# Decode attention on one core: one matmul for the score mask, one for a head's q block, and the q block written by VectorE

## The chip, the core and the metric

The kernel runs on one core of a Trainium2 chip. Its time is the device time of one execution in microseconds (us): the median of several runs. The matrix engine is TensorE (PE in the profile, its weight loads PEld), VectorE is DVE, ScalarE is ACT, GpSimd is POOL, and SyncE (SP) issues nearly all transfers.

## What is computed

Four sequences (B = 4), one new token each, go through attention over a cached window, a gated feed-forward layer, the same attention again, and the feed-forward layer again, all with the same weights. Cut to what matters:

```python
# D = 512, 32 query heads on 8 KV heads (rep = 4), head size 128, window W = 2048 of 8192, F = 1792
x = x + A(layernorm(x))
x = x + B(layernorm(x))
x = x + A(layernorm(x))
x = x + B(layernorm(x))

def A(x):
    q = (x @ wq).reshape(B, 1, 32, 128)
    k, v = the last 2048 rows of k_cache, v_cache, each KV head for 4 query heads
    p = softmax(q @ k^T * 128 ** -0.5)
    return (p @ v) @ wo

def B(x):
    return (sigmoid(x @ w_gate) * (x @ w_up)) @ w_down
```

The caches and weights are bfloat16. The two attention layers share K, V and the weights, so K (16 MB) is read once and stays on the chip until the second layer has used it; V, wq, wo and the feed-forward weights are read for each layer, apart from a few tiles that are kept.

## The kernel before

**Storage and transfers.** `arena` holds 50 slots of 512 KB, `side` one more. K takes 32 of them. Every load names a slot; a slot that is given back by its last reader is handed to the next load in a fixed list, and SyncE issues the loads in that order (`dma`, L401), each behind a semaphore wait for that reader. So a late matmul can hold up a load, and all loads behind it on SyncE's queue.

**Order of work.** Each step is recorded by `P.op` with an engine, a name, a planned duration and what it reads and writes. `_schedule` then orders the steps of each engine by a simulated time made from the planned durations (`c_dve(n)` is 130 + 1.04 n ns for VectorE, `c_act(n)` 180 + 0.833 n ns for ScalarE), so a change of a step's engine or duration may reorder others. From the second attention on (`P.chain`), TensorE keeps the order of the program; VectorE, ScalarE and GpSimd are still ordered by the planner. Steps that touch one PSUM bank from different engines wait for each other (`banks`).

**A head's scores.** `q_unit` makes the q block of a KV head: `qh` holds a head's q for 4 sequences and 4 query heads in 32 rows, and the block `qbd` needs it spread so that the group of 32 partitions `a` holds only its own columns, with zeros elsewhere. Before, four matmuls (L875), each against a window of `eyew` (an identity of 32 columns inside zeros), write four interleaved column sets of one PSUM bank (`CB`), and ScalarE copies the 256 columns to `qbd` as bfloat16 (L880). `softmax_unit` then writes the mask (L905): four matmuls of 32 output partitions each put -1e30 into the columns that do not belong to a row; sixteen score matmuls (L916) add onto it. VectorE takes the row maximum (`mx`, L929), swaps halves (L933), combines (L937, L941), and ScalarE does the exponential (L944). `turn_p` permutes the probabilities with a matmul (L957), copies them (ScalarE, L959) and transposes them (VectorE, L964).

**First attention** (`attn_first`): VectorE turns K in place first, four transposes of about 1.2 us for each head (`k_transpose`, L887); scores run two heads ahead of the product with V (`pv_unit`, L1006).

**Second attention** (`attn_second`): K is already turned. `qx(u)` calls `q_unit` for the u-th head, `score(u, between)` emits mask, `between` and scores, and gives the head's K slots back to the pool. The loop over u runs, for each head: product with V (`pv_wide`, L1088), permutation of the next head (L957), `back(u-1)` (L1123), mask and scores of head u+3, the row maximum of head u+2, `sum_up(u+1)` (L1064, L1066), `qx(u+4)` and the output projection (`wo_wide`, L1142). On VectorE each product with V is followed by `tv` (L1097), `rd` (L1102) and `sh` (L1104). GpSimd then makes `av` (L1106, L1109).

**The last feed-forward layer** (`glu`): 16 matmuls each for w_gate and w_up (L1379), the transposes (L1388), `gh` (L1406) and, against `hT`, the w_down matmuls (L1420) on three loads that are the last in the list; then a copy (L1431) and the store.

Of the kernel before, what the change touches and what calls it, by code (L numbers as in the profile page):

```python
# [278 lines left out]
def build(nc, A_x, A_k, A_v, A_wq, A_wo, B_wg, B_wu, B_wd, out, cfg=None):  # L279
# [23 lines left out]
    NR = 4 * REP  # L303
# [21 lines left out]
    with es:  # L325
        def sb(name, shape, dt):
            return es.enter_context(nc.sbuf_tensor(name, shape, dt))
# [7 lines left out]
        one, inv_d, sres, psm, nmax = (small[:, a:b] for a, b in ((0, 1), (1, 2), (2, 4), (4, 6), (6, 12)))  # L335
        s3, msk_m = small[:, 12:15].bitcast(BF16), small[:, 15:16].bitcast(BF16)
        maskp, lnr, lnd, lnv, msks = (small[:, a:b] for a, b in ((16, 20), (20, 28), (28, 32), (32, 36), (36, 58)))
        eyew = sb("eyew", [128, 224], BF16)
        perm = sb("perm", [128, 128], BF16)
        sel_b = sb("sel_b", [128, NR], BF16)  # L340
        sel_r = sb("sel_r", [128, 2 * REP], F32)
        maskr = sb("maskr", [128, 32], F32)
        msk_s = sb("msk_s", [128, 32], BF16)
        rinv = sb("rinv", [128, 2 * NR], F32)
        onb = sb("onb", [128, 2 * NR], BF16)
        onp = sb("onp", [128, 2 * REP * NR], BF16)
# [45 lines left out]
        def c_dve(n, rate=None):  # L392
            return tm["dve_fix"] + n * (tm["dve_f32"] if rate is None else rate)

        def c_act(n):
            return tm["act_fix"] + n * tm["act_el"]
# [247 lines left out]
                                       base=0, channel_multiplier=-1),  # L644
             r=[("ones_f",)], w=[("e", 0)])
        P.op("gpsimd", "inv_d", 100.0, lambda g: g.memset(inv_d[:], 1.0 / D), w=[("inv_d",)])
        P.op("gpsimd", "eyew0", 200.0, lambda g: g.memset(eyew[:], 0.0), w=[("eyew0",)])
        P.op("vector", "zero_o", 1100.0, lambda v: v.memset(ps[:, OBS[0]:WB + 1, :], 0.0), w=[("o0",)], banks=OBS + (WB,))
        P.op("vector", "zero_perm", 100.0, lambda v: v.memset(perm[:], 0.0), w=[("perm",)])
        P.op("gpsimd", "qbd0", 1800.0, lambda g: g.memset(qbd[:], 0.0), w=[("q", k2) for k2 in range(2)])  # L650
# [1 line left out]
        for jh in range(2):  # L652
            for bp in range(2):
                for i in range(2):
# [7 lines left out]
                         r=[("ones_f",), ("e", 0), ("perm",)], w=[("perm", jh, bp, i)])  # L662
        perms = [("perm", jh, bp, i) for jh in range(2) for bp in range(2) for i in range(2)]
        P.op("gpsimd", "msk_s", 200.0,
             lambda g: g.affine_select(msk_s[:, :].rearrange("p (i y) -> p i y", i=2),
                                       ones_f[:, :].rearrange("p (i y) -> p i y", i=2),
                                       [[1, 2], [0, NR]], ALU.is_equal, 0.0, base=-1, channel_multiplier=1),
             r=[("ones_f",), ("e", 0)], w=[("msk_s",)])
        P.op("vector", "msk_s2", 100.0, lambda v: v.tensor_scalar(msk_s[:, :], msk_s[:, :], -1.0e30, None, ALU.mult),
             r=[("msk_s",)], w=[("msk_s",)])  # L670
# [9 lines left out]
             lambda v: v.tensor_reduce(sel_r[:, :], sel_f[:, :].rearrange("p (g y) -> p y g", g=2), AXX, ALU.add),  # L680
             r=[("sel_f",), ("e", 0)], w=[("sel_r",)])
        P.op("vector", "eyew", 200.0,
             lambda v: v.tensor_reduce(eyew[:, 96:128], ident.rearrange("p (a j) -> p j a", a=4), AXX, ALU.max),
             r=[("e", 0), ("eyew0",)], w=[("eyew",)])
        P.op("vector", "maskp", 200.0,
             lambda v: v.tensor_reduce(maskp[:, :], ident.rearrange("p (a j) -> p a j", a=4), AXX, ALU.max),
             r=[("e", 0)], w=[("maskp",)])
        P.op("vector", "maskb", 100.0,
             lambda v: v.tensor_reduce(maskb[:, :], maskp[:, :].rearrange("p (j b) -> p b j", j=2), AXX, ALU.max),
             r=[("maskp",)], w=[("maskb",)])  # L690
        ey = eyew[:, 96:128]
        P.op("vector", "maske", 100.0,
             lambda v: v.tensor_reduce(maske[:, :], ey.rearrange("p (e m) -> p e m", m=REP), AXX, ALU.max),
             r=[("eyew",)], w=[("maske",)])
# [5 lines left out]
                                       mod4[:, :].unsqueeze(2).broadcast_to([128, REP, 2]),  # L700
                                       maskp[:, 0:2].unsqueeze(1).broadcast_to([128, REP, 2]), ALU.mult),
             r=[("mod4",), ("maskp",)], w=[("selm",)])
        P.op("vector", "selw", 100.0, lambda v: v.tensor_copy(selw[:, :], eyew[:, 96:96 + NB]), r=[("eyew",)], w=[("selw",)])
        P.op("vector", "permo", 500.0,
             lambda v: v.tensor_copy(permo[:, :].rearrange("p (m r v) -> p m r v", m=REP, r=REP),
                                     ident.rearrange("p (v m) -> p m v", m=REP).unsqueeze(2).broadcast_to([128, REP, REP, 32])),
# [159 lines left out]

        def q_unit(tag, h, k2):
            hh = h % 4
            src = qh[32 * hh:32 * hh + 32, h // 4 * 64:h // 4 * 64 + 64].rearrange("p (x r) -> p x r", r=REP)
            dst = ps[:, CB, 0:256].rearrange("p (x y) -> p x y", y=NR)  # L870

            def e_qx(pe):
                last = None
                for a in range(4):
                    last = pe.matmul(dst[:, :, a * REP:(a + 1) * REP], eyew[32 * hh:32 * hh + 32, 96 - 32 * a:224 - 32 * a],  # L875
                                     src, start=True, stop=True)
                return last
            P.op("tensor", "qx" + tag, 250.0, e_qx, r=[("qh", h // 4), ("eyew",)], w=[("cb",)], banks=(CB,))
            P.op("scalar", "qe" + tag, c_act(256),
                 lambda a: a.copy(qbd[:, k2 * 256:(k2 + 1) * 256], ps[:, CB, 0:256]),  # L880
                 r=[("cb",)], w=[("q", k2)], banks=(CB,))

        def k_transpose(h):
            need(("K", h))
# [9 lines left out]
        def softmax_unit(tag, hk, wait=False, q=True, between=None):  # L894
            u = ucount[0]
            ucount[0] += 1
            k2 = u % 2
            bank, pt = {HKV: (OBS[0], 2), HKV + 1: (WB, 3)}.get(u, (SB[k2], k2))
            if q:
                q_unit(tag, hk, k2)  # L900

            def e_m(pe):
                last = None
                for gi in range(4):
                    last = pe.matmul(ps[32 * gi:32 * gi + 32, bank, :], msk_s[:, :],  # L905
                                     msk_m[:, :].unsqueeze(1).broadcast_to([128, 256, 2]), start=True, stop=False)
                return last

            def e_s(pe):
                last = None if wait else e_m(pe)  # L910
                for cp in range(4):
                    for gi in range(4):
                        jh, bp = gi // 2, gi % 2
                        kt = kpair(hk, bp).rearrange("p (j c k t) -> p c t j k", c=2, k=32, t=2)
                        q0 = ((k2 * 4 + cp) * 2 + bp) * 32
                        last = pe.matmul(ps[32 * gi:32 * gi + 32, bank, :], qbd[:, q0:q0 + 32],  # L916
                                         kt[:, cp // 2, cp % 2, jh * NJ:(jh + 1) * NJ, :], start=False, stop=(cp == 3))
                return last
            if wait:
                P.op("tensor", "M" + tag, 4 * tm["pe_row"], e_m, r=[("msk_s",), ("msk_m",)], w=[("pss", pt)], banks=(bank,))  # L920
                if between is not None:
                    between()
            P.op("tensor", "S" + tag, (16 if wait else 20) * tm["pe_row"], e_s,
                 r=[("msk_s",), ("msk_m",)] + [("slot", 4 * hk + t) for t in range(4)] + [("q", k2)],
                 w=[("pss", pt)], banks=(bank,))
            def soft():
                mk = mxt[:, k2 * 32:(k2 + 1) * 32]
                P.op("vector", "mx" + tag, c_dve(512),
                     lambda v: v.tensor_reduce(nmax[:, k2:k2 + 1], ps[:, bank, :], AXX, ALU.max),  # L929
                     r=[("pss", pt)], w=[("mx", k2)], banks=(bank,))  # L930
# [305 lines left out]
        def attn_second():  # L1236
# [8 lines left out]
            def qx(u):  # L1245
                if u < HKV:
                    q_unit(tag(u), hs[u], u % 2)

            def score(u, between=None):
                if u >= HKV:  # L1250
                    return
                softmax_unit(tag(u), hs[u], True, False, between)
                if u == 0:
                    soft(0)
                for bp in range(2):
                    pool.release(4 * hs[u] + 2 * bp)
                fill()
# [5 lines left out]
            def sum_up(u):  # L1263
                if u < NW:
                    sums(tag(u), u % 2)
                elif u < HKV:
                    sums_old(tag(u), u % 2)

            qx(0)
            score(0, lambda: q_mms(1, 0, OBS[1], (1,)))  # L1270
            qx(1)
            score(1)
            turn(0)
            qx(2)
# [299 lines left out]
```

## Time and profile before

| what | value |
|---|---|
| runs of the kernel before | 177.63, 177.19, 177.51 us; median 177.51 |
| the profiled execution | 177.0 us, of which the profile's span is 175.3 |
| busy share of the span | PE 60%, DVE 60%, ACT 19%, POOL 13% |
| loads | 70.00 MB, mean 399 GB/s |
| instructions on PE | 1661 matmuls and 1661 weight loads |

The span runs from the first instruction to the last of one execution; 1.7 us of that execution's own time lie around it. The profiled execution is 0.5 us shorter than the median of the runs. A busy share is a mean over stages with different limits; a row such as "L905 PE MATMUL" belongs to line 905 of the kernel before.

### The profile page before, as it was taken

The numbers are of one execution on the slowest core, as the hardware profiler recorded it, in microseconds if no ns is written. First come the engines' busy times: TensorE is split into PE (matmuls) and PEld (weight loads), VectorE is DVE, ScalarE is ACT, GpSimd is POOL, SyncE is SP. The second block draws the span as 40 slices with busy tenths as digits, with TensorE's granted clock in tenths as the row PEclk, the third lists the DMA queues.
The fourth block names the chain that finished last, engine by engine and source line by source line (L and its number), as shares of the span: only waits on it lengthen the run. The fifth ranks groups of instructions, "written<-read, shape, count | busy, mean of one in ns | idle before, by whom it ended". The sixth has DMA issues, their size and how long they took to land.

```text
span 175.3 us, 3927 instructions
## 1 busy us (share of the span) xinstructions
PE 105.7 (60%) x1661; PEld 54.7 (31%) x1661; DVE 104.4 (60%) x257; ACT 32.7 (19%) x87; POOL 22.2 (13%) x90
## 2 busy tenths in 40 slices
PE   0536246259566273661765456547977999776673
PEld 0203112014334041340445452142322444445321
DVE  6307997994957738378322381316299999751351
ACT  2002031322303003021030000100143455430011
POOL 6100010101101001010010000000011453442000
PEclk9999999999999999999999999999999999995555
DMA  5999999999999999999999999999999999999980
GB/s 188 426 426 426 426 419 424 408 421 423 419 419 412 420 424 426 421 405 427 419 419 415 415 400 407 402 410 403 394 413 404 423 419 424 421 416 423 419 344 25
DMA packets 12226, 70.00 MB, mean 399 GB/s; under 512 B 1320, under 2 KB 1328, under 8 KB 6064
## 3 DMA queue, kind: packets, MB, share of 16 engines
q1 hardware_dynamic: 12200, 69.74, 97.1%
q8 instruction: 13, 0.21, 0.5%
q14 instruction: 5, 0.04, 0.1%
q10 hardware_dynamic: 8, 0.00, 0.0%
HBM read 69.73 MB, written 0.00 MB: 398 GB/s over the span
## 4 chain that ended last, share of the span: by engine, by line
DMA 52%; DVE 24%; PE 19%; issue 2%; SPq 1%; ACT 0%; DVEq 0%
DMA arena<-in_A_v_cache_dram 20%; DMA arena<-in_B_w_down_dram 18%; DVE arena L887 12%; DMA arena<-in_A_wq_dram 10%; PE ps L916 8%; DMA arena<-in_B_w_gate_dram 5%; DVE small L929 3%; PE ps L905 3%; PE ps L1088 2%; DVE small L933 1%; DVE arena L593 1%; PE ps L1006 1%; DVE side L937 1%; PE ps L828 1%; DVE small L941 1%
## 5 line engine op out<-in xcount | busy, mean ns | idle before, releaser
L887 DVE STREAM_TRANSPOSE arena<-arena 128x1024 f32<-128x1024 f32 x32 | 37.0, 1205 | 0.1
L1006 PE MATMUL ps<-side,arena 128*128 128x8 bf16 x576 | 18.2, 168 | 14.1 <-DMA arena<-in_A_v_cache_dram 14.0
L916 PE MATMUL ps<-arena,side 128*32 128x512 bf16 x256 | 25.0, 524 | 0.1
L1006 PEld LDWEIGHTS ps<-side,arena 128*128 128x128 bf16 x576 | 16.7, 104 | 20.5 <-DMA arena<-in_A_v_cache_dram 18.8
L929 DVE TENSOR_REDUCE small<-ps 128x1 f32<-128x512 f32 x16 | 10.8, 676 | 17.6 <-PE ps L916 17.5
L944 ACT ACTIVATE side<-ps,small 128x512 bf16<-128x512 f32 x16 | 11.0, 687 | 36.8 <-PE ps L1024 18.3
L905 PE MATMUL ps<-small,msk_s 128*32 128x512 bf16 x64 | 8.4, 512 | 13.9 <-DVE arena L887 13.1
L880 ACT CAST side<-ps 128x256 bf16<-128x256 f32 x16 | 5.9, 370 | 34.4 <-PE ps L916 25.4
L959 ACT CAST side<-ps 128x512 bf16<-128x512 f32 x16 | 9.4, 586 | 10.8 <-PE ps L957 10.8
L916 PEld LDWEIGHTS ps<-arena,side 128*32 128x32 bf16 x256 | 8.2, 119 | 10.0 <-issue 7.2
L973 POOL CAST small<-small 128x1 bf16<-128x1 f32 x9 | 1.7, 188 | 76.1 <-ACT side L944 76.1
L957 PE MATMUL ps<-side,perm 128*128 128x512 bf16 x16 | 7.9, 494 | 5.2 <-ACT side L944 5.2
L828 PE MATMUL ps<-arena,xn 128*4 128x512 bf16 x60 | 7.5, 572 | 3.9 <-DMA arena<-in_A_wq_dram 3.6
L784 ACT ACTIVATE small<-ps 128x4 f32<-128x4 f32 x4 | 0.7, 174 | 48.1 <-PE ps L780 48.1
L1379 PE MATMUL ps<-arena,xn 128*4 128x448 bf16 x60 | 7.2, 549 | 3.3 <-DMA arena<-in_B_w_up_dram 1.5
L964 DVE STREAM_TRANSPOSE side<-side 128x256 f32<-128x256 f32 x16 | 6.9, 433 | 2.0 <-ACT side L959 1.8
L875 PE MATMUL ps<-side,eyew 32*128 32x64 bf16 x64 | 5.6, 217 | 3.4 <-ACT side L880 2.4
L1088 PE MATMUL ps<-arena,side 128*32 128x512 bf16 x112 | 7.3, 381 | 0.2 <-DVE small L941 0.2
L1014 DVE TENSOR_TENSOR onb<-ps,rinv 128x16 bf16<-128x16 f32 x9 | 1.7, 185 | 9.0 <-PE ps L1006 8.8
L905 PEld LDWEIGHTS ps<-small,msk_s 128*32 128x32 bf16 x64 | 1.7, 97 | 16.8 <-DVE arena L887 15.4
L1388 DVE STREAM_TRANSPOSE side<-ps 128x448 f32<-128x448 f32 x4 | 2.6, 650 | 7.3 <-PE ps L1379 7.3
L840 DVE STREAM_TRANSPOSE side<-ps 128x512 f32<-128x512 f32 x3 | 2.1, 716 | 7.9 <-PE ps L828 7.8
(123 smaller groups left out, 137.8 us busy)
## 6 DMA issues: line engine op xcount, KB each, us to landing
arena<-in_A_v_cache_dram SPq DMA_DIRECT2D x27, 1024.0 KB, 18.8
arena<-in_A_k_cache_dram SPq DMA_DIRECT2D x16, 1024.0 KB, 24.9
arena<-in_A_wq_dram SPq DMA_DIRECT2D x4, 1024.0 KB, 7.8
arena<-in_A_wo_dram SPq DMA_DIRECT2D x3, 1024.0 KB, 26.5
arena<-in_A_wq_dram SPq DMA_DIRECT2D x6, 512.0 KB, 6.3
arena<-in_B_w_up_dram SPq DMA_DIRECT2D x4, 448.0 KB, 6.1
arena<-in_B_w_gate_dram SPq DMA_DIRECT2D x2, 896.0 KB, 21.7
arena<-in_B_w_up_dram SPq DMA_DIRECT2D x2, 896.0 KB, 23.9
```

What stands on the lines that cost most here:

```text
L828: last = pe.matmul(ps[32 * hh:32 * hh + NB, qb, :], xn[:, c * NB:(c + 1) * NB], src[:, o + hh * 512:o + (hh + 1) * 512], start=(c == 0), s ...
L887: P.op("vector", "T%d_%d" % (h, t), c_dve(1024), lambda v, v32=v32: v.transpose(v32, v32), r=[("slot", 4 * h + t)], w=[("slot", 4 * h + t)])
L905: last = pe.matmul(ps[32 * gi:32 * gi + 32, bank, :], msk_s[:, :], msk_m[:, :].unsqueeze(1).broadcast_to([128, 256, 2]), start=True, stop= ...
L916: last = pe.matmul(ps[32 * gi:32 * gi + 32, bank, :], qbd[:, q0:q0 + 32], kt[:, cp // 2, cp % 2, jh * NJ:(jh + 1) * NJ, :], start=False, s ...
L929: lambda v: v.tensor_reduce(nmax[:, k2:k2 + 1], ps[:, bank, :], AXX, ALU.max),
L944: lambda a: a.activation(prow[:, :].rearrange("p (m x t) -> p m x t", x=32, t=2), ps[:, bank, :].rearrange("p (m t x) -> p m x t", x=32, t ...
L957: lambda pe: pe.matmul(ps[:, pb, :], perm[:, :], prow[:, :], start=True, stop=True),
L959: P.op("scalar", "pc" + tag, c_act(512), lambda a: a.copy(prow[:, :], ps[:, pb, :]), r=[("ppb", pb)], w=[("prow",)], banks=(pb,))
L964: P.op("vector", "pt" + tag, c_dve(256), lambda v: v.transpose(et, prow[:, :].bitcast(F32)), r=[("prow",)], w=[("e", k2)])
L1006: last = pe.matmul(ps[:, ob, bp * 8:bp * 8 + 8], src[:, j * 128:(j + 1) * 128], ev[:, j % 2, j % 16 // 2, x0:x0 + 8], start=(j == 0), stop ...
L1088: last = pe.matmul(ps[32 * g:32 * g + 32, ob, :], ew[:, g, mq, t], src.rearrange("p (m t d) -> p t m d", t=2, d=128)[:, t], start=(n == 0) ...
L1379: last = pe.matmul(ps[32 * g:32 * g + NB, gub[n], 0:NF], xn[:, c * NB:(c + 1) * NB], src[:, g * NF:(g + 1) * NF], start=(c == 0), stop=(c ...
```

## The change

1. **Mask**: the selector `msk_s` is 128 columns wide (four copies of the 32), and the four mask matmuls of a head become one with 128 output partitions.
2. **q block**: the windowed `eyew` gives way to `eye4`, four copies of the 32-column identity side by side. One matmul of 64 columns puts the q of a head into all four groups of 32 partitions, and VectorE, not ScalarE, writes the 256 columns of `qbd`: it multiplies the 64 columns, repeated four times, by `maskp`, which is 1 where the partition group is the column's own.
3. **Order in the second attention**: `qx(1)` stands in `score(0)` behind the mask and one q matmul step, ahead of the first head's scores, where it stood behind them.
4. **Setup**: the GpSimd memset of `eyew` goes, a VectorE copy that fills `eye4` comes, and the select of `msk_s` is four times as wide.

```diff
-        eyew = sb("eyew", [128, 224], BF16)
+        eye4 = sb("eye4", [128, 128], BF16)
-        msk_s = sb("msk_s", [128, 32], BF16)
+        msk_s = sb("msk_s", [128, 128], BF16)
...
         def q_unit(tag, h, k2):
             hh = h % 4
-            src = qh[32 * hh:32 * hh + 32, h // 4 * 64:h // 4 * 64 + 64].rearrange("p (x r) -> p x r", r=REP)
-            dst = ps[:, CB, 0:256].rearrange("p (x y) -> p x y", y=NR)
-
-            def e_qx(pe):
-                last = None
-                for a in range(4):
-                    last = pe.matmul(dst[:, :, a * REP:(a + 1) * REP], eyew[32 * hh:32 * hh + 32, 96 - 32 * a:224 - 32 * a],
-                                     src, start=True, stop=True)
-                return last
-            P.op("tensor", "qx" + tag, 250.0, e_qx, r=[("qh", h // 4), ("eyew",)], w=[("cb",)], banks=(CB,))
-            P.op("scalar", "qe" + tag, c_act(256),
-                 lambda a: a.copy(qbd[:, k2 * 256:(k2 + 1) * 256], ps[:, CB, 0:256]),
-                 r=[("cb",)], w=[("q", k2)], banks=(CB,))
+            src = qh[32 * hh:32 * hh + 32, h // 4 * 64:h // 4 * 64 + 64]
+            dst = ps[:, CB, 0:64]
+            P.op("tensor", "qx" + tag, 150.0,
+                 lambda pe: pe.matmul(dst, eye4[32 * hh:32 * hh + 32, :], src, start=True, stop=True),
+                 r=[("qh", h // 4), ("eye4",)], w=[("cb",)], banks=(CB,))
+            P.op("vector", "qe" + tag, c_dve(256),
+                 lambda v: v.tensor_tensor(
+                     qbd[:, k2 * 256:(k2 + 1) * 256].rearrange("p (x a r) -> p x a r", a=4, r=REP),
+                     dst.rearrange("p (x r) -> p x r", r=REP).unsqueeze(2).broadcast_to([128, NR, 4, REP]),
+                     maskp[:, :].unsqueeze(1).unsqueeze(3).broadcast_to([128, NR, 4, REP]), ALU.mult),
+                 r=[("cb",), ("maskp",)], w=[("q", k2)], banks=(CB,))
...
             def e_m(pe):
-                last = None
-                for gi in range(4):
-                    last = pe.matmul(ps[32 * gi:32 * gi + 32, bank, :], msk_s[:, :],
-                                     msk_m[:, :].unsqueeze(1).broadcast_to([128, 256, 2]), start=True, stop=False)
-                return last
+                return pe.matmul(ps[:, bank, :], msk_s[:, :],
+                                 msk_m[:, :].unsqueeze(1).broadcast_to([128, 256, 2]),
+                                 start=True, stop=False, skip_group_check=True)
...
+            def ahead():
+                q_mms(1, 0, OBS[1], (1,))
+                qx(1)
+
             qx(0)
-            score(0, lambda: q_mms(1, 0, OBS[1], (1,)))
-            qx(1)
+            score(0, ahead)
             score(1)
```

More of the change, by code (lines that the diff above doesn't have):

```diff
@@ L646, in build @@
         P.op("gpsimd", "inv_d", 100.0, lambda g: g.memset(inv_d[:], 1.0 / D), w=[("inv_d",)])
-        P.op("gpsimd", "eyew0", 200.0, lambda g: g.memset(eyew[:], 0.0), w=[("eyew0",)])
         P.op("vector", "zero_o", 1100.0, lambda v: v.memset(ps[:, OBS[0]:WB + 1, :], 0.0), w=[("o0",)], banks=OBS + (WB,))
@@ L664, in build @@
         P.op("gpsimd", "msk_s", 200.0,
-             lambda g: g.affine_select(msk_s[:, :].rearrange("p (i y) -> p i y", i=2),
-                                       ones_f[:, :].rearrange("p (i y) -> p i y", i=2),
-                                       [[1, 2], [0, NR]], ALU.is_equal, 0.0, base=-1, channel_multiplier=1),
+             lambda g: g.affine_select(msk_s[:, :].rearrange("p (g i y) -> p g i y", g=4, i=2),
+                                       ones_f[:, :].rearrange("p (i y) -> p i y", i=2).unsqueeze(1).broadcast_to([128, 4, 2, NR]),
+                                       [[0, 4], [1, 2], [0, NR]], ALU.is_equal, 0.0, base=-1, channel_multiplier=1),
              r=[("ones_f",), ("e", 0)], w=[("msk_s",)])
@@ L682, in build @@
         P.op("vector", "eyew", 200.0,
-             lambda v: v.tensor_reduce(eyew[:, 96:128], ident.rearrange("p (a j) -> p j a", a=4), AXX, ALU.max),
-             r=[("e", 0), ("eyew0",)], w=[("eyew",)])
+             lambda v: v.tensor_reduce(eye4[:, 0:32], ident.rearrange("p (a j) -> p j a", a=4), AXX, ALU.max),
+             r=[("e", 0)], w=[("eyew",)])
+        P.op("vector", "eye4", 150.0,
+             lambda v: v.tensor_copy(eye4[:, 32:128].rearrange("p (a j) -> p a j", j=32),
+                                     eye4[:, 0:32].unsqueeze(1).broadcast_to([128, 3, 32])),
+             r=[("eyew",)], w=[("eye4",)])
         P.op("vector", "maskp", 200.0,
@@ L690, in build @@
              r=[("maskp",)], w=[("maskb",)])
-        ey = eyew[:, 96:128]
+        ey = eye4[:, 0:32]
         P.op("vector", "maske", 100.0,
@@ L702, in build @@
              r=[("mod4",), ("maskp",)], w=[("selm",)])
-        P.op("vector", "selw", 100.0, lambda v: v.tensor_copy(selw[:, :], eyew[:, 96:96 + NB]), r=[("eyew",)], w=[("selw",)])
+        P.op("vector", "selw", 100.0, lambda v: v.tensor_copy(selw[:, :], eye4[:, 0:NB]), r=[("eyew",)], w=[("selw",)])
         P.op("vector", "permo", 500.0,
@@ L916, in e_s @@
                         last = pe.matmul(ps[32 * gi:32 * gi + 32, bank, :], qbd[:, q0:q0 + 32],
-                                         kt[:, cp // 2, cp % 2, jh * NJ:(jh + 1) * NJ, :], start=False, stop=(cp == 3))
+                                         kt[:, cp // 2, cp % 2, jh * NJ:(jh + 1) * NJ, :], start=False, stop=(cp == 3),
+                                         skip_group_check=True)
                 return last
```

## The prediction

> **What bounds it now.** I read the page first (busy shares, 40 slices, chain), then the chain of waits at its end, sums by stage, and the timeline of VectorE and TensorE where the change acts.
>
> ```profile
> PE 105.7 (60%) x1661; PEld 54.7 (31%) x1661; DVE 104.4 (60%) x257; ACT 32.7 (19%) x87; POOL 22.2 (13%) x90
> ...
> DMA  5999999999999999999999999999999999999980
> ...
> DMA 52%; DVE 24%; PE 19%; issue 2%; SPq 1%; ACT 0%; DVEq 0%
> ```
>
> No engine is over 60%, while the transfers are busy from the first slice to the last but one: 70 MB at some 420 GB/s set the time. The chain's end, from 146 us on, names the load:
>
> ```profile
> 146.35 25.46 DMA arena<-in_B_w_down_dram
> ...
> 171.86 0.59 PE ps L1420 x8
> ...
> 172.49 0.41 PE ps L1420 x6
> ```
>
> The last w_down parts land at 171.82 and 172.44, and matmuls, copy and store follow. So an earlier finish of the computation is worth nothing; a later one costs whatever exceeds its cover. Next, the stages (columns: us, then busy time of PE, PEld, DVE, ACT, POOL with counts, clock, DMA share, GB/s):
>
> ```profile
> 122.96:126.62 3.66, 3.66 (x35) 1.23 (x36) 0.31 (x2) 0.37 (x1) 0.00 (x0) 1.00 1.01 392
> 126.62:149.55 22.93, 20.48 (x293) 8.56 (x292) 21.42 (x66) 10.58 (x29) 7.30 (x21) 1.00 1.01 416
> 149.55:162.60 13.05, 8.96 (x183) 6.31 (x179) 5.95 (x19) 3.85 (x10) 4.98 (x15) 0.81 1.01 419
> ```
>
> From the first row maximum (126.62) to 149.55, the second attention, VectorE is busy 21.42 of 22.93 us. One head of it, VectorE then TensorE (start, duration):
>
> ```profile
> 143.28 0.65 DVE L929 TENSOR_REDUCE small<-ps 128x1 f32<-128x512 f32 x1
> 143.85 0.18 DVE L1066 RECIPROCAL arena<-ps 64x8 f32<-64x8 f32 x1
> ...
> 146.24 0.45 DVE L964 STREAM_TRANSPOSE side<-side 128x256 f32<-128x256 f32 x1
> 146.61 0.65 DVE L929 TENSOR_REDUCE small<-ps 128x1 f32<-128x512 f32 x1
> ...
> 144.93 0.40 PE L905 MATMUL ps<-small,msk_s 128*32 128x512 bf16 x4
> 145.16 1.08 PE L916 MATMUL ps<-arena,side 128*32 128x512 bf16 x16
> ...
> 146.38 0.28 PE L875 MATMUL ps<-side,eyew 32*128 32x64 bf16 x4
> 146.60 0.39 PE L1142 MATMUL ps<-arena,opb 128*4 128x512 bf16 x4
> ```
>
> A head takes 3.33 us (143.28 to 146.61). VectorE's ten steps fill it: where the next step doesn't need the one before, it starts 0.08 early (143.85 against 143.93); where it does, 0.03 late. Nothing waits for another engine. TensorE is full too, and its next V product starts at 146.83, 0.14 after L964, which it needs, has ended at 146.69. Two engines without slack: work moved from the one to the other lengthens the head.
>
> **The change, part by part.**
>
> *Mask.* The four mask matmuls stand abreast: the scores start 0.23 after them (144.93 to 145.16), about what four score matmuls take of a head's sixteen (1.08 / 4 = 0.27). One matmul of the same 512 columns streams as long: I take 0 saved, bounds -0.05 and +0.09, since behind the one full-width 512-column matmul of the head (L957) the next starts 0.32 after (144.48 to 144.80). The Trainium skill ("TensorEngine Tiling (Array Packing)", Key Properties) says that changing the tiling mode drains the engine, and one wide mask ahead of 32-column scores is one more change; no row here shows that pair. By it TensorE's head would be some 0.1 us longer, and the sum 0.5 us more over six heads only if TensorE were the bound.
>
> *q block on TensorE.* Four matmuls hold it 0.22 (146.38 to 146.60); one some 0.1 (two of L1123 hold it 0.13): 0.12 saved a head. TensorE's head becomes 3.33 - 0.12 = 3.21.
>
> *q block on VectorE.* ScalarE loses 16 copies of 0.37 (L880), which nothing in this stage waits for. VectorE gains 16 multiplies of 128x256 from PSUM. The nearest row has the same mask, form and types with 64 elements:
>
> ```profile
> L1029 DVE TENSOR_TENSOR onp<-ps,small x9: 224/225/225, 45.1 to 161.7; 128x64 bf16<-128x64 f32 x9
> ```
>
> From it to L929 (512 elements, 0.65) is 0.95 ns an element, so 256 take 0.225 + 192 x 0.95 ns = 0.41; bounds 0.22 and 0.65. Between independent steps that adds 0.41 - 0.08 = 0.33 to 0.35; between dependent ones it also fills their gap, some 0.24. I take 0.35: q blocks become ready just when L929 and L1066 run, which do not depend on each other. Bounds 0.14 (0.22 - 0.08) and 0.57.
>
> *Where these 16 lie.* Eight are in the first attention: 8 x 0.35 = 2.8 us on a VectorE that is the chain there. Cover: VectorE idles 2.4 us before a row maximum in each of heads 3 to 7, and the loads are issued 20 us ahead of landing until 67 us, still 7.7 at 85.94; the V products of the last heads wait for V (landing 86.78, 91.73, 99.18). I put this at 0; were that cover gone, up to 2.8. Of the second attention's eight, q blocks 0 and 1 fall into 123.4 to 126.6, where VectorE stands idle; six (2 to 7) fall into the full stretch: 6 x 0.35 = 2.1 us. Their cover is none: VectorE's work there only adds up. Behind each on VectorE's queue stand L933 to L964, for which the exponential (ScalarE), the next V product (TensorE) and GpSimd's L1106 wait.
>
> *Order.* qx(1) ahead of the first scores puts them 0.1 to 0.2 later (one cold matmul; the four took 0.30, 123.52 to 123.82): 0.15. The second head's scores lose their wait for the copy (126.93 to 127.30) and end some 0.4 earlier, but VectorE reaches them only at 131.96: 0. SP's queue: the V load that waits for the first scores is issued 0.15 later (126.61, 3.4 us ahead of the landing before it), the next ones 0.4 earlier. All loads up to 153 us shift by at most 2.2 us, with 5 to 20 us of queue ahead: 0 at the end.
>
> *Setup.* Steps of 0.1 to 0.3 us before 7 us; the last wq part lands at 13.05: 0.
>
> *Sum.* The second attention's VectorE work ends 0.15 + 2.1 = 2.25 us later. From there (sh of the fifth head, 149.37) to its end at 162.60 the steps wait for each other through L1109, L1123, L1142 and L1088 with no wait for a load on that path (the last V product's second half waits for L1109, not for V landed at 159.36), so 2.25 passes on whole. Cover of the last layer: w_up's third part of matmuls waited for its load until 168.16, but TensorE was free at about 167.83: 0.33. hT is ready at 170.01; w_down could start at 170.1. Its first twelve of 14 steps of four matmuls (0.10 each: 32 matmuls in 1.02 with a tail of 0.31) need 1.3 with pauses and must be through by 172.49: a start by 171.15 costs nothing, so 1.05 more. Cover 1.38. Net 2.25 - 1.38 = +0.87. The profiled execution's 177.0 becomes 177.9; the runs' median stands 0.5 above it: 178.4.
>
> **The rivals.**
>
> *A, the cover holds.* The six multiplies go between dependent steps (0.24 each), or less: 0.15 + 1.45 = 1.6, net +0.2: 177.7. For it: five of a head's ten boundaries are dependent ones. Against: the planner places by readiness, not by gaps. It decides below 1.9 us of delay.
>
> *B, faster: the last load lands earlier.* The packets show that w_down's first of 16 parts lands at 170.01, the last at 172.44: one DMA engine trails, having lost 1.6 us to each of two 16 KB instruction loads of TensorE's (30.5 and 132.5). 96 fewer matmuls and weight loads each are 0.75 of such a load fewer. If only that engine is spared, the next sets the end, 0.27 earlier; if the five that trail most are (parts from 171.83 on), the sixth does, at 171.06: 1.4 earlier. Middle: 176.7. Against: 0.75 of a load shifts the second hit at 132.5 only by half the interval to the next load (143.68).
>
> *C, slower still: q block 2 comes late.* If the planner puts it behind L840 and L844 (131.03 to 132.04), the third head's scores wait for it, and behind them on TensorE its first V product, on which VectorE's L1097 waits: 1.0 us of VectorE idle on top: 179.4. Decides if VectorE runs out of other steps (about 2.6 us of them against 2.4 of TensorE's).
>
> *D, the clock.* Sixteen score matmuls take 1.93 us before 126.6 and 1.08 after; PEclk reads 0.81 in 149.55 to 162.60 and 0.50 behind. If full rate ends earlier, the seventh V product (L1088, 1.05) and the copies beside it run at half rate: +1.0 on the same path: 179.4. The Trainium skill ("TensorE: Matmul & The Clock Gate", Part 1) says the rate falls after an idle window of some 3.4 us that runs free of the kernel; the rows agree that it falls in the sparse tail.
>
> **How the numbers follow.** A measurement of this kernel tells about 0.3% (0.5 us) from no change. Forecast 0.50: with 0.24 to 0.45 a multiply, delay 1.6 to 2.9, net +0.2 to +1.5; of it 0.43 beyond 0.3%, 0.07 within. A 0.16, within. B 0.14: 0.12 beyond, 0.02 within. C 0.15 and D 0.05, slower. Faster 0.12, same 0.25, slower 0.63. The likeliest is 178.4; its own range 177.7 to 179.0. The range for 8 in 10 goes down into B (177.2) and up past C (179.6), which takes in a multiply of up to 0.55.
>
> **What would show it.** Right: a new VectorE row of some 0.41 us x16; the head's period in the second attention at 3.6 to 3.7 instead of 3.33; the attention's end 2 us past 162.60; w_down's first matmul after 170.64, waiting for hT instead of its load; w_down still landing near 172.4; mask to scores still 0.2 to 0.3. Wrong: an unchanged period; a landing moved by over 0.5; VectorE idle for TensorE in that stretch (C).

## The result, and the profile after

The changed kernel takes 178.92 us in the median (178.16 to 180.28, 11 runs) beside 177.51 (176.97 to 178.45, 11 runs) of the kernel before on the same chip: a ratio of 1.0085, interval 1.0062 to 1.0108, so 1.4 us slower. Its profiled execution took 178.35 us with a span of 176.6, against 177.0 and 175.3. Line numbers from here on are those of the changed kernel unless a run is named: L878 is the multiply, L904 the mask, L915 the scores, L1409 makes hT, L1423 is w_down.

The page first (busy shares, the DMA row of the 40 slices, the chain by engine, and the new row of costliest groups):

```profile
PE 105.7 (60%) x1565; PEld 52.3 (30%) x1565; DVE 110.1 (62%) x274; ACT 27.3 (15%) x71; POOL 22.0 (12%) x89
...
DMA  5999999999999999999999999999999999999970
...
DMA 46%; DVE 26%; PE 15%; SPq 8%; issue 3%; ACT 1%; POOL 1%; POOLq 0%; DVEq 0%
...
L878 DVE TENSOR_TENSOR side<-ps,small 128x256 bf16<-128x256 f32 x16 | 6.1, 382 | 1.2 <-PE ps L875 1.2
```

VectorE is busy 5.7 us more, ScalarE 5.4 less. The transfers are as full as before, yet a smaller part of the chain is theirs. The chain's last steps tell why (start, duration, engine, tile, line):

```profile
171.81 0.54 DVE side L1391
172.37 0.23 DVE rinv L1409
172.73 1.50 PE ps L1423 x56
174.25 0.28 DVE side L1434
```

Before, two rows of w_down matmuls followed two landings of loads. Now all 56 steps run in one go at 172.73, and they start behind VectorE's L1409: the computation ends last. The last w_down part lands at 172.65 (172.44 before), so the loads have hardly moved.

Next the second attention in two stretches, cut near the place where the prediction cut the kernel before (columns as there). The first one ends behind VectorE's last multiply, not at the same step: the fifth head's `sh` (L1104), with which the stretch before closed at 149.37, starts at 151.37.

```profile
127.12:149.80 22.68, 19.66 (x230) 7.04 (x229) 21.43 (x65) 7.84 (x20) 6.96 (x20) 1.00 1.02 420
149.80:165.40 15.60, 10.69 (x199) 6.93 (x198) 8.38 (x26) 4.52 (x12) 5.33 (x17) 0.83 1.01 418
```

VectorE's full stretch no longer ends near 149.6: it reaches into the second row, where VectorE is busy 8.38 of 15.60 us, for 5.95 of 13.05 before. One head, VectorE then TensorE:

```profile
141.20 0.21 DVE L941 TRANSPOSE_TENSOR_REDUCE small<-side 128x1 f32<-128x32 f32 x1
141.34 0.16 DVE L1066 RECIPROCAL arena<-ps 64x8 f32<-64x8 f32 x1
141.42 0.36 DVE L878 TENSOR_TENSOR side<-ps,small 128x256 bf16<-128x256 f32 x1
141.71 0.67 DVE L929 TENSOR_REDUCE small<-ps 128x1 f32<-128x512 f32 x1
...
145.31 0.67 DVE L929 TENSOR_REDUCE small<-ps 128x1 f32<-128x512 f32 x1
...
142.74 0.39 PE L904 MATMUL ps<-small,msk_s 128*128 128x512 bf16 x1
143.06 1.11 PE L915 MATMUL ps<-arena,side 128*32 128x512 bf16 x16
144.10 0.28 PE L1064 MATMUL ps<-arena 128*64 128x8 f32 x2
144.31 0.20 PE L875 MATMUL ps<-side,eye 32*128 32x64 bf16 x1
144.44 0.39 PE L1142 MATMUL ps<-arena,opb 128*4 128x512 bf16 x4
```

The multiply starts at 141.42 and the next step at 141.71: it overlaps both neighbours and takes 0.3 us of VectorE's time. The head takes 3.60 (141.71 to the next L929 at 145.31) instead of 3.33, so its period grows by 0.27. The attention's last step and the casts behind the last w_down matmul in the kernel before, and the same last step in the changed one:

```profile
162.60 0.22 DVE L1333 TENSOR_REDUCE xT<-ps 128x16 f32<-128x64 f32 x1 [0.69 <-PE ps L1195]
172.92 0.61 DVE L1431 CAST side<-ps 4x128 bf16<-4x128 f32 x2 [2.91 <-PE ps L1420]
...
165.49 0.23 DVE L1336 TENSOR_REDUCE xT<-ps 128x16 f32<-128x64 f32 x1 [0.69 <-PE ps L1195]
```

The attention's last step is 2.89 later. The casts start at 174.25 instead of 172.92: of the 2.89, 1.33 reach the end.

### The profile page after: what moved, and what is told of

Its sections match the earlier page's. It is cut to its first block, busy times and chain, and to the rows that moved or that the text cites. A ratio compares the mean times of both kernels' runs of the same rounds, so it can differ in the third digit from the quotient of the medians.

```text
span 176.6 us, 3742 instructions
## 1 busy us (share of the span) xinstructions
PE 105.7 (60%) x1565; PEld 52.3 (30%) x1565; DVE 110.1 (62%) x274; ACT 27.3 (15%) x71; POOL 22.0 (12%) x89
## 4 chain that ended last, share of the span: by engine, by line
DMA 46%; DVE 26%; PE 15%; SPq 8%; issue 3%; ACT 1%; POOL 1%; POOLq 0%; DVEq 0%
DMA arena<-in_A_v_cache_dram 34%; SPq L401 8%; DVE arena L888 5%; DMA arena<-in_B_w_gate_dram 5%; PE ps L915 4%; DMA arena<-in_A_wq_dram 4%; DMA arena<-in_B_w_down_dram 3%; DVE small L929 3%; PE ps L1006 3%; DVE arena L1097 3%; DVE side L964 2%; DVE arena L1102 2%; DVE side L937 2%; DVE arena L593 1%; PE ps L1382 1%
## 5 line engine op out<-in xcount | busy, mean ns | idle before, releaser
L915 PE MATMUL ps<-arena,side 128*32 128x512 bf16 x256 | 25.8, 539 | 0.2 <-DVE side L878 0.2
L929 DVE TENSOR_REDUCE small<-ps 128x1 f32<-128x512 f32 x16 | 10.9, 681 | 14.5 <-PE ps L915 14.5
L904 PE MATMUL ps<-small,msk_s 128*128 128x512 bf16 x16 | 8.4, 522 | 14.1 <-DVE arena L888 10.3
L957 PE MATMUL ps<-side,perm 128*128 128x512 bf16 x16 | 8.0, 498 | 9.3 <-ACT side L944 9.3
L915 PEld LDWEIGHTS ps<-arena,side 128*32 128x32 bf16 x256 | 6.4, 114 | 12.9 <-issue 10.3
L1088 PE MATMUL ps<-arena,side 128*32 128x512 bf16 x112 | 7.3, 380 | 0.0
L843 DVE STREAM_TRANSPOSE side<-ps 128x512 f32<-128x512 f32 x3 | 2.2, 717 | 7.9 <-PE ps L831 7.8
L878 DVE TENSOR_TENSOR side<-ps,small 128x256 bf16<-128x256 f32 x16 | 6.1, 382 | 1.2 <-PE ps L875 1.2
L904 PEld LDWEIGHTS ps<-small,msk_s 128*128 128x128 bf16 x16 | 1.6, 101 | 16.6 <-DVE arena L888 11.0
L957 PEld LDWEIGHTS ps<-side,perm 128*128 128x128 bf16 x16 | 1.6, 100 | 14.5 <-ACT side L944 14.0
```

Of the source, the lines that this page charges most:

```text
L904: return pe.matmul(ps[:, bank, :], msk_s[:, :], msk_m[:, :].unsqueeze(1).broadcast_to([128, 256, 2]), start=True, stop=False, skip_group_c ...
L957: lambda pe: pe.matmul(ps[:, pb, :], perm[:, :], prow[:, :], start=True, stop=True),
```

## The experiments

Each run is compared with the kernel before on its own chip (medians 177.20 to 177.46), so ratios are what can be compared between them. Theory 1 is the prediction's forecast: six multiplies in VectorE's full stretch delay the attention, and the last layer's wait for its loads covers a part. Its rivals: the mask's one matmul, the order, the first attention's multiplies.

**Which of the parts costs the time.** Three kernels keep the mask, the order and the single q matmul, and give the block to ScalarE where VectorE is to be spared (shortened; SPOT stands for the condition of each kernel):

```diff
-            P.op("vector", "qe" + tag, c_dve(256), ... ALU.mult)
+            if SPOT:      # never / first attention only / second attention only
+                P.op("vector", "qe" + tag, c_dve(256), ... ALU.mult)
+            else:
+                for x in range(4):
+                    a.activation(qbd...[:, :, x, :], dst..., ACTF.Copy, scale=maskp[:, x:x + 1])
```

Multiply nowhere on VectorE:

> No multiply on VectorE at all: ScalarE writes the block of all sixteen heads as four scaled copies of 64 columns. Mask, order and the single q matmul as after. Theory 1: 177.2 to 177.8 us, as before; period 3.33, seventh tv near 157.0 to 157.3 (the first mx still 0.3 late), first matmul of w_down bound by its load again. Rival 2 (mask) and rival 3 (order): 178.9, as after.

In the first attention only:

> VectorE's multiply in the first attention alone (eight); in the second attention the same block is written by ScalarE as four copies of 64 columns, each scaled by one column of the mask (estimate 0.2 us each, from the 16-column copy's 0.182, so ScalarE has about 2.5 us of work in a head's 3.33). Mask and order as after. Theory 1: the second attention has its period of 3.33 again, the attention ends near 162.9, the loads set the end: 177.3 to 177.8 us, as before. Rival 2 (mask) and rival 3 (order): 178.9, as after. Rival 4 (the first attention's eight multiplies delay what loads wait for): 178.9, as after.

In the second only:

> VectorE's multiply in the second attention alone; in the first attention ScalarE writes the block as four scaled copies of 64 columns. Mask and order as after. Theory 1: 178.7 to 179.1 us, as after; period 3.6. Rival 4 (the first attention's multiplies cost it): 177.5, as before. Rivals 2 and 3 (mask, order): 178.9, as after, so this run doesn't tell them from theory 1.

Measured: nowhere 177.52 us, ratio 1.0021 (0.9994 to 1.0048); first only 177.66, 1.0013 (0.9992 to 1.0034); second only 178.85, 1.0081 (1.0050 to 1.0112). With the second attention spared, its head is back at 3.33 and w_down waits for its load again; with the first one spared nothing is won. So the loss is the second attention's multiplies, and neither the mask, nor the order, nor the first attention's eight. One detail was missed: without any multiply on VectorE the first mx came at 127.92 and not 0.3 late. That is a landing of wq in that execution: TensorE waited 1.67 us for it ahead of the first block, for 0.67 in the changed kernel. The attention then ended at 163.79, 1.19 late, and w_down still waited for its load.

**What the order is for.** First the q block alone, with the old mask and the old order (shortened, against the kernel before):

```diff
+            P.op("vector", "qe" + tag, ...)   # and one qx matmul; mask and order as before
```

> The q block alone is changed: one matmul and VectorE's multiply, while the mask stays four matmuls of 32 columns and qx(1) stays behind the first mask and scores. Theory 1 (VectorE's multiply in the full stretch of the second attention costs what is lost): 178.6 to 178.9 us, as after or up to 0.3 below it, since the first mx (126.62 before, 127.12 after) should come back towards 126.8; qe 0.36 to 0.41 us a row, the seventh head's tv about 2.6 us after the 156.71 of before. Rival 2 (the mask's one matmul, with the wait of mask to scores of 0.32 instead of 0.23, costs it): 177.5, as before. Rival 3 (the order, qx(1) ahead of the first scores, costs it): 177.5, as before.

It took 181.72 us, ratio 1.0239 (1.0204 to 1.0275): slower than the whole change by 2.7 by the ratios, which none of the three theories had. Two candidates were left, the old mask and the old order; the next kernel is the whole change with the old order alone:

```diff
-            score(0, ahead)
+            score(0, lambda: q_mms(1, 0, OBS[1], (1,)))
+            qx(1)
```

> After with the order of before: qx(1) stands behind the first scores again, so the second block's multiply stands on VectorE behind the first head's mx to nm and behind the four transposes of L593 (2.47 us). Mask and q block as after. Theory 1a (part 2 alone was slow because of that place in VectorE's queue): like part 2 alone, 181.4 to 182.0 us; second mx at 133.5 to 133.8 instead of 132.58, third at 138.5 instead of 134.48, a gap in the loads behind 130 us. Rival (part 2 alone was slow for the old mask beside it): 178.9, as after.

It took 181.60 us, ratio 1.0263 (1.0221 to 1.0304): the order is the cause. The two kernels differ in the mask alone, and their intervals overlap. The timeline of that kernel, VectorE then TensorE (in brackets the idle time before a step and what ended it):

```profile
128.22 2.46 DVE L593 STREAM_TRANSPOSE arena<-ps 128x512 f32<-128x512 f32 x4
130.61 0.39 DVE L878 TENSOR_TENSOR side<-ps,small 128x256 bf16<-128x256 f32 x1
133.00 0.69 DVE L929 TENSOR_REDUCE small<-ps 128x1 f32<-128x512 f32 x1 [2.01 <-PE ps L915]
133.69 0.42 DVE L878 TENSOR_TENSOR side<-ps,small 128x256 bf16<-128x256 f32 x1
...
126.75 0.61 PE L904 MATMUL ps<-small,msk_s 128*128 128x512 bf16 x1
131.05 1.90 PE L915 MATMUL ps<-arena,side 128*32 128x512 bf16 x16 [3.69 <-DVE side L878]
```

The second head's multiply has its place in VectorE's queue behind the first head's softmax steps and four transposes (L593). TensorE has done the second mask at 127.36 and stands idle 3.69 us for that block; then VectorE stands idle 2.01 for the scores. The third multiply repeats it on a smaller scale, and the third L929 comes at 137.16 instead of 134.48. (Both the second and the third came earlier than expected: 133.00 for 133.5 to 133.8, 137.16 for 138.5.) In the sums of 122 to 140 us VectorE does 2.25 us less work, and the loads that wait for the scores' slots come late (DMA share 0.91 instead of 1.00). This kernel's row:

```profile
122.00:140.00 18.00, 13.24 (x119) 3.82 (x119) 11.86 (x31) 2.73 (x6) 1.92 (x7) 1.00 0.91 348
```

The changed kernel's:

```profile
122.00:140.00 18.00, 15.02 (x147) 4.48 (x147) 14.11 (x39) 4.17 (x10) 2.81 (x9) 1.00 1.00 402
```

The fourth corner is the order without the multiply, on the kernel before:

```diff
+            def ahead():
+                q_mms(1, 0, OBS[1], (1,))
+                qx(1)
             qx(0)
-            score(0, lambda: q_mms(1, 0, OBS[1], (1,)))
-            qx(1)
+            score(0, ahead)
```

> Before with the order of after alone: qx(1) ahead of the first scores; mask, four q matmuls and ScalarE's copy as before. Theory 1: the first mx 0.1 to 0.3 us later, all of it under the cover of the last layer's loads: 177.2 to 177.7 us, as before; so the order has its worth only where VectorE writes the block. Rival (the order by itself saves time, as the third head's scores come earlier): under 176.9.

177.68 us, ratio 1.0009 (0.9985 to 1.0033): no gain by itself. The first mx came at 127.82, 1.2 late and not 0.1 to 0.3: 0.71 of it stood already at the last wq part's matmuls (123.67 for 122.96), and the other 0.49 is the order with four q matmuls, more than expected. The attention ended 1.39 late, at 163.99, and the loads still set the end. In the kernel before the old order costs nothing, since ScalarE's copy does not stand in the queue of the softmax steps.

**How much a multiply costs, and the cover.** Twice the multiply from the third head on:

```diff
             P.op("vector", "qe" + tag, ...)
+            if tag[0] == "2" and tag not in ("2.0", "2.1"):
+                P.op("vector", "q2" + tag, ...)   # the same multiply again
```

> After, with the multiply of the heads from the third on done twice in the second attention (the same numbers are written again). Theory 1 (a multiply takes 0.30 us of VectorE's time in the full stretch, and after has no cover left): six more by 0.30 are 1.8, so 180.5 to 180.9 us, the head's period 3.9, w_down's first matmul again behind the step of L1409. Rival (the loads or the clock set after's time, VectorE has slack): 178.9 to 179.3.

180.21 us, ratio 1.0177 (1.0131 to 1.0223). VectorE's steps in a head (in this kernel L885 is the second multiply and L1104 the head's `tv`):

```profile
138.90 0.36 DVE L878 TENSOR_TENSOR side<-ps,small 128x256 bf16<-128x256 f32 x1
139.30 0.42 DVE L885 TENSOR_TENSOR side<-ps,small 128x256 bf16<-128x256 f32 x1
139.64 0.70 DVE L1104 STREAM_TRANSPOSE arena<-ps 128x512 f32<-128x512 f32 x1
```

The two take 0.74 together (138.90 to 139.64), because the second writes the same tile and waits for the first: 0.40 and 0.34, not 0.30 each. The head is 4.03, 0.43 more; six of these, less 0.65 of a stretched step that is told below and is missing here, are 1.9. The seventh tv (first V copy of the seventh head) comes at 161.47, 1.87 behind the changed kernel, and the span is 2.1 longer; by the ratios it is 1.6 us. Time follows VectorE's delay about one to one here, which the rival denied. The time is 0.3 below the band, on a chip whose kernel before is 0.3 faster too.

The other way, with the last three heads' blocks on ScalarE:

```diff
+            if tag[0] == "0" or int(tag[2:]) < 5:   # VectorE's multiply, else ScalarE's four copies
```

> VectorE's multiply in the first attention and for the first five heads of the second (three of them in its full stretch), ScalarE's four scaled copies for the last three heads. Theory 1 with the cover of 1.56 us: delay of the attention's end 0.3 to 0.5 from the start and 3 by 0.30, 1.2 to 1.4, all under the cover, so 177.3 to 177.8 us, as before (with a stretched L937 on top up to 178.1). Rival (no cover: each of the six multiplies costs its sixth of the loss from the first on): half of the loss stays, 178.1 to 178.3.

177.71 us, ratio 1.0026 (1.0006 to 1.0045). The attention ends at 163.99, 1.39 late as expected, and the list of TensorE's waits at the end (us in total, times, longest) starts as before:

```profile
PE ps L1433 <- DMA arena<-in_B_w_down_dram: 1.4, 2, 1.1
```

So 1.4 us of delay leaves the loads last (L1433 is w_down in that kernel). The cover can be read from every profile whose end is the computation's: the attention's delay less that of the casts is 2.89 - 1.33 = 1.56 for the changed kernel, 3.06 - 1.33 = 1.73 with the multiply in the second attention only, 2.30 - 0.87 = 1.43 with the short product below, 4.77 - 3.41 = 1.36 with the doubled multiply, 5.83 - 4.46 = 1.37 with the old order. These differ because the run of 56 w_down matmuls does; for the changed kernel, the multiply in the second attention only, and the old order it is:

```profile
172.73 1.47 PE L1423 MATMUL ps<-arena,rinv 128*4 128x128 bf16 x56 [0.67 <-DVE rinv L1409]
172.90 1.29 PE L1433 MATMUL ps<-arena,rinv 128*4 128x128 bf16 x56 [0.67 <-DVE rinv L1419]
175.66 1.66 PE L1420 MATMUL ps<-arena,rinv 128*4 128x128 bf16 x56 [0.67 <-DVE rinv L1406]
```

The clock granted during these runs was 0.62, 0.71 and 0.50. With the doubled multiply the run took 1.66 (0.50), with the short product 1.60 (0.58). Cover and run add up to 3.02 or 3.03 in all five, so where the computation ends last, up to 0.4 us of the end hangs on the clock that these matmuls happen to get. In the kernel with three blocks on ScalarE the waits decide for the cover; its time alone would not, since half of the loss, 1.004, still lies in its interval.

**Relieving VectorE.** Three kernels take the copy of the upper half (L1104, 0.18 us a head) off VectorE:

```diff
-            P.op("vector", "sh" + tag, ..., lambda v: v.tensor_copy(osh[0:64, :], o32[64:128, :]), ...)
+            P.op("scalar", "sh" + tag, ..., lambda a: a.copy(osh[0:64, :], o32[64:128, :]), ...)
```

On the changed kernel:

> After, with the same copy (L1104) moved to ScalarE. Theory 1 (after is bound by VectorE with 1.33 us beyond the cover): six copies by 0.20 are 1.2 off, so 177.5 to 177.9 us, near before; seventh tv near 158.4 for 159.60. Rival (mask or landing sets after's time): 178.9, as after.

On the kernel before:

> Before, with the copy of the upper half (its line 1101, 0.18 us and 0.02 of gap on VectorE a head) moved to ScalarE. Theory 1 (in before the last loads set the end, VectorE's stretch has 1.56 us of cover): VectorE's seventh tv about 1.2 us earlier (155.5 for 156.71), the time unchanged: 177.2 to 177.6. Rival (VectorE sets the end in before too, and the change simply adds to it): 1.2 less, 176.2 to 176.4.

With the copy left out, on the kernel that multiplies in the first attention only:

> The run with VectorE's multiply in the first attention alone, less the copy of the upper half in the second attention (L1104; the upper half of the V products' sum is left out, the lower is added to itself), so VectorE has 0.20 us a head less to do than before, and TensorE keeps the single mask and q matmuls. Theory 1 (the last loads set the end as soon as VectorE's stretch is short enough): seventh tv 1.0 to 1.2 us earlier than the 157.02 of that run, time unchanged at 177.3 to 177.8 us. Rival (VectorE sets the end throughout): 1.2 less, 176.3 to 176.5.

On the changed kernel: 178.07 us, 1.0030 (1.0003 to 1.0057), about 1.0 us off by the ratios, with the seventh tv at 158.04 (158.4 expected): 0.2 above the band, near it. On the kernel before: 177.75, 1.0027 (1.0001 to 1.0053), no gain, but also no earlier tv (157.84, not 155.5; the first mx was 0.63 late), so it says nothing of the floor. Its head is 3.30 where VectorE's work is about 3.33 - 0.20 = 3.13: VectorE now waits for the scores. TensorE had 15.21 busy us of 15.40 in 134.60 to 150.00 of the kernel before already. And the seventh V product was slow:

```profile
155.88 1.90 PE L1088 MATMUL ps<-arena,side 128*32 128x512 bf16 x16
```

It takes 1.05 in the kernels before and after; the granted clock in 150 to 160 us was 0.76 here and 0.88 before. The third kernel took 177.77, 1.0033 (1.0013 to 1.0053), and its seventh tv stayed at 157.05. Its head is 3.33 still, with VectorE waiting:

```profile
143.87 0.69 DVE L939 TENSOR_REDUCE small<-ps 128x1 f32<-128x512 f32 x1 [0.24 <-PE ps L925]
```

So near 3.33 VectorE is no longer what sets a head; TensorE's steps fill it as well. In the kernel that multiplies in the first attention only, TensorE is busy for all 9.97 us of three heads (140.28 to 150.25). The expectation of an earlier tv failed in both, and what a shorter attention would do to the end was not tried in any run; no version here beats the kernel before.

**The stretched step.** Six multiplies by 0.30 are 1.8, but tv of the seventh head came 2.39 late from the first mx on. The trace shows the rest at L937, which took 0.25 us elsewhere, beside GpSimd's product:

```profile
147.85 0.66 POOL L1109 TENSOR_TENSOR arena<-arena 64x256 bf16<-64x256 f32 x1
148.13 0.43 DVE L937 SCALAR_TENSOR_TENSOR side<-small,maskr 128x32 f32<-128x32 f32 x1
...
151.95 0.72 DVE L937 SCALAR_TENSOR_TENSOR side<-small,maskr 128x32 f32<-128x32 f32 x1
151.96 0.66 POOL L1109 TENSOR_TENSOR arena<-arena 64x256 bf16<-64x256 f32 x1
```

Both times L937 ends 0.05 behind L1109 (148.56 and 148.51; 152.67 and 152.62). The test cuts the product short:

```diff
-                     av[0:64, :].rearrange("p (x q e) -> p x q e", x=8, q=4), ...   # [64, 8, 4, 8]
+                     av[0:64, :].rearrange("p (x q e) -> p x q e", x=8, q=4)[:, 0:1], ...   # [64, 1, 4, 8]
```

> After, with GpSimd's 64x256 product (L1109, 0.66 us a head) cut to its first eighth, 64x32: seven eighths of the attention's values in the second attention are left out. Nothing of VectorE's, TensorE's or ScalarE's changes. Theory P (L937 was stretched from 0.25 to 0.43 and 0.72 us by GpSimd's product beside it): L937 at 0.25 us in all heads, or up to 0.4 where it meets another GpSimd step, seventh tv 0.5 to 0.65 us earlier, 178.2 to 178.5 us. Rival (L937 was late for its own operands): L937 unchanged at 0.43 and 0.72 in the sixth and seventh of its rows, 178.9.

178.17 us, ratio 1.0058 (1.0025 to 1.0090). The same two rows in that kernel:

```profile
147.80 0.24 POOL L1109 TENSOR_TENSOR arena<-arena 64x32 bf16<-64x32 f32 x1
148.08 0.25 DVE L937 SCALAR_TENSOR_TENSOR side<-small,maskr 128x32 f32<-128x32 f32 x1
...
151.72 0.75 DVE L937 SCALAR_TENSOR_TENSOR side<-small,maskr 128x32 f32<-128x32 f32 x1
151.73 0.24 POOL L1109 TENSOR_TENSOR arena<-arena 64x32 bf16<-64x32 f32 x1
151.93 0.50 POOL L802 TENSOR_SCALAR_AFFINE_SELECT side<-small 128x384 bf16<-128x384 f32 x1
```

The first is back at 0.25. The second stays at 0.75, but now another GpSimd step, L802, stands beside it, and L937 again ends 0.04 behind that one's end (152.47 and 152.43). The rival expected both unchanged. So a GpSimd step beside it holds L937, and it need not be the product; that L937 in turn holds GpSimd, no row here shows. The gain was only partly what was expected (seventh tv 0.19 earlier instead of 0.5 to 0.65, another 0.40 between it and the attention's end, where the product itself is on the chain). The time alone would not decide, as the interval takes in the changed kernel's 1.0085; the rows do. Where the steps fall decides: with the doubled multiply L937 took 0.25 in every head, with L1104's copy on ScalarE in the changed kernel 0.61, 0.62 and 0.39 in three of them.

## Why the prediction was right, point by point

*Bound and mechanism.* As forecast: VectorE's full stretch grew, the attention ended later, the cover of the last layer's loads took a part of that, and w_down's first matmul now waits for hT and not for its load.

*Mask.* Taken as 0 within -0.05 and +0.09; the wait from mask to scores is 0.32 (142.74 to 143.06) for 0.23, the upper end. The Trainium skill's rule ("TensorEngine Tiling (Array Packing)", Key Properties), that a change of tiling mode drains the engine, agrees with this 0.09; no run here separates a drain from the wider matmul itself. It costs nothing, as TensorE has slack now: in 134.60 to 150.00 its permutation (L957) waits five times for the exponential, 1.8 us in all, for 0.4 in one wait before.

*q block on TensorE.* Forecast 0.12 saved a head, measured 0.09: 0.13 (144.31 to 144.44) for 0.22. With the mask's 0.09 that leaves nothing: TensorE's own head stays near 3.33 where the prediction had 3.21: it fills the heads of the kernel that multiplies in the first attention only, and without the copy the head is no shorter.

*q block on VectorE.* The row was forecast at 0.41 and is 0.382 in the mean. Added time was forecast at 0.35 and is 0.30 between two starts (0.27 by the head's period), so six give 1.6 to 1.8 for 2.1. The first attention's eight cost nothing, as the kernel that spares them showed.

*Start.* 0.15 was mis-sized: the first mx came 0.50 late, of which 0.23 is a later wq landing in this execution; 0.27 is left for the order.

*Missing term.* L937's 0.65 in the sixth and seventh rows was not foreseen; the sum of delay is 0.50 + 1.8 + 0.65 = 2.95 (2.8 by the period) beside 2.89 measured, where the prediction had 2.25.

*Cover.* 1.38 forecast, 1.56 by this profile (2.89 - 1.33), 1.4 to 1.7 over five. At the clock of 0.50, which the prediction read in the kernel before, it is 1.36 and 1.37, as forecast; the changed kernel's matmuls met 0.62. Net 1.33 for 0.87: the forecast of 178.4 was 0.5 low, by the missing term and not by the mechanism.

*Luck.* Part of the hit is errors that offset each other. The start and the missing term alone would have moved the forecast by 0.35 + 0.65 to 179.4, outside its own range of 177.7 to 179.0; the cheaper multiplies and the larger cover took some 0.5 of it back.

*Order.* The largest gap in the working: it counts 0.15 and an unused gain. The price of doing without it is about 3 us (ratios of 1.0239 and 1.0263 for 1.0085). Rival C had the mechanism, a q block late in VectorE's queue with TensorE and then VectorE idle, and looked for it at block 2; it lies at block 1 in the old order, and the change avoids it. In the changed kernel block 2 is written at 131.36, ahead of L843, and nothing stalls.

*The other rivals.* A (cover holds) fails with 2.89 of delay against 1.9. B fails: the last landing moved by 0.2. D (clock) did not happen here, with 0.83 granted behind 149.80 and 1.05 for the seventh V product; what it describes did show, at 0.85 us, in the profiled execution of the relieved kernel before.

What stays open: the kernels in which the loads set the end again lie 0.1 to 0.3% above the kernel before, with last landings at 172.9 to 174.0 in their profiled executions (172.44 before, in an execution 0.5 below its median). Whether they are a few tenths slower, and why, was not taken apart.

## What to carry to other kernels

Work that is moved to the engine whose steps stand back to back costs its time between two starts, not its duration, and only what exceeds the cover behind it: find both before counting busy time. When a step moves to another engine, look at what already stands in that engine's queue ahead of its new place, and who waits: here a wrong place cost about twice what the multiplies cost in the right one. And relief of one engine buys nothing where a second is as full: count both before moving.

## What the runs showed of the hardware

VectorE's L937, which takes two operands from SBUF, is held by a GpSimd step beside it until that step ends: 0.25 us became 0.43, 0.72 and 0.75, each ending 0.04 to 0.05 behind the GpSimd step. The Trainium skill ("SBUF — State Buffer", Who interferes with whom) states such an exclusive lock, for a VectorE instruction with two SBUF inputs against a GpSimd instruction that reads SBUF; the trace agrees for L937 as the one held. Recorded starts a hundredth apart don't tell which of the two that is: at 151.95 L937's record starts 0.01 ahead of GpSimd's, and yet it is L937 that is held.

In the profiled execution of the kernel before with `sh` on ScalarE, with less on VectorE and no more on TensorE, the seventh V product took 1.90 us instead of 1.05, at a granted clock of 0.76 instead of 0.88 in 150 to 160 us. That is one execution; whether the relief brings it on each time was not looked at.

The same 56 matmuls of w_down took 1.29, 1.47, 1.60 and 1.66 us at granted clocks of 0.71, 0.62, 0.58 and 0.50, in kernels that do the same work there.
